# Pooled attention and routed experts on one core: 64-row transposes in two row groups, and indirect transfers tied to the place of the products

## The chip, the cores and the metric

One Trainium2 chip, of which the kernel uses one core. The metric is the device time of one execution in microseconds (us). The engines are TensorE (PE, with its weight loads listed apart as PEld), VectorE (DVE), ScalarE (ACT), GpSimd (POOL) and SyncE (SP, which only issues transfers).

## The reference

```
q_pool = q.reshape(8, 8, 576, 2, 64).mean(axis=3)          # 8 batches, 8 heads, 1152 rows of 64
scores = q_pool @ k.T / 8;  attn = softmax(scores)
x      = (attn @ v) -> [4608 tokens, 512]                  # 8 batches x 576, heads side by side
e, g   = argmax and top softmax of x @ w_gate              # 8 experts
out[t] = g[t] * relu(x[t] @ w1[e]) @ w2[e]                 # w1 512x1024, w2 1024x512
```

## The kernel before, in words

**Attention.** The work goes by batch (8), by pair of heads (4) and by half of the 576 pooled rows (2). `load_pair` brings K, Q and V of a pair (`kn`, `qn`, `vn`), ACT reorders K (`kp`), POOL adds neighbouring rows of Q (`qp`, L465), and `piece` turns both on PE. A pair has four pieces: five tiles of Q, four of K, four of K, and one of each. Each takes the only slot of the PSUM kind `bank`, turns 128x128 (K) or 96x128 (Q) tiles through the identity, and is copied out by ACT into `kT` (L489) and `qT` (L493). `scores` multiplies `kT` by `qT` for nine chunks of K, each into one of two PSUM slots of the kind `st` (L521, four tile products of 64x64 at a time), DVE takes them to `s` (L525), ACT makes the exponential (L553), POOL folds the chunks for the sums (L599), `values` multiplies `s` by V (L624). Score and value products run "tiled", in 64x64 pieces of the array; PE's transposes of K and Q and the gate products are not.

**Routing.** At the end of a batch each token's expert is found, and POOL writes the tokens' entries into one list for each expert with six indirect transfers (`enlist`, `lists<-re,di`, L799).

**MoE.** 16 lists of tokens are worked off, the first two of 384 tokens ("early") from what the first seven batches found, so that their tokens are gathered while the last batch is still in the attention. POOL gathers 32 tokens at a time (`gather`, `xr` or `xq` `<-x_runs,ix`, L899, 148 in all), DVE weighs them (L1056, L1057) and transposes them (L1060), ACT and DVE split them into a high and a low part (L1064, L1019), PE does the first products (L1113, `ph`) and the second ones (L1141, `py`), ACT copies `y`, and POOL scatters it to the output (`out_dram<-y,rec`, L1148, 41).

**Order.** None of this is written in the order in which it runs. Each step is added to a `Flow` with an engine, a length, a due key, what it follows and what buffers it holds; `Flow.emit` walks these with a model of time, and `trace` writes the instructions of all engines in the order that it finds. The tile framework adds the waits that the data need, and it takes two indirect scatters to the same output for dependent unless they are declared free of each other. An engine works off its own instructions in the written order and waits at each for its semaphores.

Of the kernel before, what the change touches and what calls it, by code (L numbers as in the profile page):

```python
# [25 lines left out]
COLS, QUADS = 1, 2  # L26
# [38 lines left out]
SWITCH = 150  # L65

# [22 lines left out]
class Flow:  # L89


    def __init__(self, room=None, old=(), new=(), swap=None):

        self.room, self.steps = room, []
        self.old, self.new, self.swap = set(old), set(new), swap

    def add(self, eng, ns, fn, key=0.0, after=(), holds=(), tiled=False, late=0):
# [5 lines left out]
        step = [key, len(self.steps), eng, ns, fn, list(holds), 0, [], True, list(after), tiled, late]  # L103
# [6 lines left out]
    def carry(self, eng, ns, fn, key, after, holds, move, late=0):  # L110

        s = self.add(eng, ns, fn, key, after, holds)
        return s and self.add("DMA2" if eng == "POOL" else "DMA", move, lambda: None, key, [s], holds, late=late + (1200 if eng == "POOL" else 0))

    def emit(self):
# [12 lines left out]
        tiled, blocked = False, {}  # L128
# [23 lines left out]
        while left:  # L152
            moved = False
            for e in free:
# [44 lines left out]
                free[e] = start + s[3]  # L199
                heapq.heappush(events, (free[e] + OWN[e], s[1], 0, s))  # L200
# [29 lines left out]
    def trace(self, order):  # L230

        todo = sum(self.uses(s, self.old) for s in order)
        while order:
# [5 lines left out]
            for s in order:  # L239
# [6 lines left out]
                s[4]()  # L246
# [6 lines left out]
def kernel(  # L253
# [166 lines left out]
    def act(n):  # L420
        return 110 + 0.833 * n
# [23 lines left out]
    def load_pair(o, f, key, b, hp):  # L445
# [3 lines left out]
        qn = tile_of(o, "qn", [QP, 2, NJ, 2, D], pool=o.ld)  # L449
        x.vn = vn = tile_of(o, "vn", [P, 2, NC, D], bufs=3, pool=o.rt)  # L450
        kp = tile_of(o, "kp", [P, NC, 2, D], pool=o.ld)
        qp = tile_of(o, "qp", [QP, NJ, 2, D], pool=o.ld)
# [8 lines left out]
        q0 = f.carry("SP", 480, lambda: load(qn.t, qb), key + K_LOAD, (), [qn], 2600)  # L461
# [11 lines left out]

        def piece(key, ks, qs, after):

            pt = bank(o)
            nk, n = len(ks) * P, len(ks) * P + len(qs) * QP

            def turn():
                for i, c in enumerate(ks):  # L480
                    nc.tensor.transpose(pt.t[:, i * P:(i + 1) * P], kp.t[:, c].rearrange("p h d -> p (h d)"), ident)
                for i, j in enumerate(qs):
                    nc.tensor.transpose(pt.t[:, nk + i * QP:nk + (i + 1) * QP], qp.t[:, j].rearrange("p h d -> p (h d)"),
                                        ident[:QP, :QP])

            s = f.add("PE", 0.9 * n, turn, key, after, [pt, *([kT, kp] if ks else []), *([qT, qp] if qs else [])])
            o.turned.append(s)
            if ks:
                e = f.add("ACT", act(nk) - 44, lambda: nc.scalar.copy(kT.t[:, ks[0] * P:ks[0] * P + nk], pt.t[:, :nk]),  # L489
                          key, done(s), [pt, kT])  # L490
                x.k.update((c, done(e)) for c in ks)
            if qs:
                e = f.add("ACT", act(n - nk) - 44, lambda: nc.scalar.copy(qT.t[:, qs[0] * QP:qs[0] * QP + n - nk], pt.t[:, nk:n]),  # L493
                          key, done(s), [pt, qT])
                for half in range(qs[0] * 2 // NJ, 2):
                    x.q[half] = x.q.get(half, []) + done(e)

        piece(key, [], [0, 1, 2, 3, 4], done(q1))
        piece(key + 2, [0, 1, 2, 3], [], done(k1))
        piece(key + 4, [4, 5, 6, 7], [], done(k1))  # L500
        piece(key + 6, [8], [5], done(k1, q1))
        return x

    def scores(o, f, key, x, half, step=None):
# [8 lines left out]
        for c in range(NC):  # L513
            pt = hold_of("st", lambda h: o.ps_s.tile([P, 2, 512], F32, **h.own("st")))

            def product(c=c, pt=pt):

                for i in range(2):
                    for h in range(2):
                        up, to = slice(h * D, (h + 1) * D), slice(i * D, (i + 1) * D)  # L520
                        nc.tensor.matmul(pt.t[to, h, :HQ], x.kT.t[up, c * P + i * D:c * P + (i + 1) * D], x.qT.t[up, cols],  # L521
                                         start=True, stop=True, tile_position=(up.start, to.start))

# [763 lines left out]
```

## Time and profile before

| what | value |
|---|---|
| median of 3 runs | 1312.04 us (1309.75 to 1315.79) |
| the profiled execution | 1304.89 us, its span 1303.3 us, mean granted PE clock 0.967 |
| PE busy | 1222.0 us, 94% of the span |
| POOL busy | 862.1 us, 66% |
| DVE busy | 771.5 us, 59% |
| ACT busy | 637.5 us, 49% |
| attention, routing and early lists | about 0 to 755 us of the span |
| MoE | about 755 to 1303 us |

Busy PE time is an average over two parts with different limits, so the prediction reads stretches of the span. Ends of matmuls are modelled and overlap the next start, so the step from one start to the next is the measure of what PE work costs.

### The profile page before, as it was taken

To read this page: it belongs to the slowest core of one execution; us is meant where nothing else is said; L and a number is where in the kernel's file an instruction comes from. 1 tells how busy PE (TensorE), PEld (TensorE's weight loads), DVE (VectorE), ACT (ScalarE), POOL (GpSimd) and SP (SyncE) were. 2 spreads that over 40 slices of the span, in tenths; PEclk is the share of its full clock that TensorE was granted. 3 is DMA by queue.
4 is the path that set the end of the run, shared out by engine and by line. 5 is a ranking of instruction groups with operands and counts; after the bars stand their busy time and mean duration, and the time that the engine had idled before them with its cause. 6 is when DMAs were issued, how large, how long until landed. Compare 5 with 4: busy or idle time off the path is not lost. (4 is left out here: it accounts for less than half of the span.)

```text
span 1303.3 us, 32720 instructions
## 1 busy us (share of the span) xinstructions
PE 1222.0 (94%) x13677; PEld 844.5 (65%) x13677; DVE 771.5 (59%) x2080; ACT 637.5 (49%) x832; POOL 862.1 (66%) x539
## 2 busy tenths in 40 slices
PE   7999999999999999999999598898689889999995
PEld 3555555555555555555555157797578779899895
DVE  5777777767767768768776067663334435425440
ACT  4666666656666666666574046332223323424440
POOL 2999799798998998998992701577475755300110
PEclk8999999999999999999999699999798899999998
DMA  5523233323333333323324205652333434414330
GB/s 165 140 82 93 87 93 94 95 74 105 98 92 110 78 93 104 85 89 98 91 77 152 50 2 140 211 167 57 108 109 96 124 91 128 128 69 146 104 100 19
DMA packets 73517, 131.75 MB, mean 101 GB/s; under 512 B 9347, under 2 KB 32799, under 8 KB 73360
## 3 DMA queue, kind: packets, MB, share of 16 engines
q1 hardware_dynamic: 62528, 109.89, 28.8%
q0 software_dynamic: 9744, 19.64, 5.4%
q8 instruction: 110, 1.80, 0.7%
q14 instruction: 47, 0.39, 0.1%
q10 hardware_dynamic: 1088, 0.03, 0.1%
HBM read 108.75 MB, written 21.02 MB: 100 GB/s over the span
## 5 line engine op out<-in xcount | busy, mean ns | idle before, releaser
L525 DVE TENSOR_SCALAR_CACHE_REDUCE s<-st 128x576 f32<-128x576 f32 x576 | 424.5, 754 | 166.9 <-PE st L521 162.6
L553 ACT ACTIVATE s<-s,bias 128x1728 f32<-128x1728 f32 x192 | 325.3, 1733 | 172.5 <-DVE bias L549 168.2
L521 PE MATMUL st<-qT,kT 64*64 64x288 f32 x4608 | 374.8, 413 | 10.1 <-DVE bias L549 4.9
L624 PE MATMUL pa<-s,vn 64*64 64x288 f32 x4608 | 357.8, 405 | 3.6 <-issue 3.5
L521 PEld LDWEIGHTS st<-qT,kT 64*64 64x64 f32 x4608 | 160.5, 133 | 135.4 <-DVE s L525 30.0
L624 PEld LDWEIGHTS pa<-s,vn 64*64 64x64 f32 x4608 | 171.8, 133 | 102.9 <-issue 9.5
L599 POOL TENSOR_TENSOR fold<-s 128x1728 f32<-128x1728 f32 x58 | 224.3, 3875 | 14.3 <-ACT s L553 9.3
L599 POOL TENSOR_TENSOR fold<-fold,s 128x1728 f32<-128x1728 f32 x58 | 224.1, 3873 | 1.1
L1113 PE MATMUL ph<-xh,w1h 128*128 128x384 f32 (+6 forms) x512 | 162.9, 318 | 31.7 <-DVE hl L1121 22.0
L1113 PE MATMUL ph<-xl,w1h 128*128 128x384 f32 (+6 forms) x512 | 161.2, 315 | 0.7 <-DVE xl L1019 0.6
L1113 PE MATMUL ph<-xh,w1l 128*128 128x384 f32 (+6 forms) x512 | 160.8, 314 | 0.0
L1148 POOL DMA_INDIRECT out_dram<-y,rec x41 | 44.0, 1072 | 174.2 <-ACT y L1153 158.3
L899 POOL DMA_INDIRECT xr<-x_runs,ix x104 | 111.4, 1072 | 65.7 <-issue 26.8
L1121 DVE SCALAR_TENSOR_TENSOR hl<-ph,hh 128x384 fp32r<-128x384 f32 (+5 forms) x100 | 54.8, 550 | 148.3 <-ACT hh L1119 114.0
L1119 ACT ACTIVATE hh<-ph 128x384 fp32r<-128x384 f32 (+5 forms) x100 | 48.8, 488 | 187.4 <-PE ph L1113 139.6
L1141 PE MATMUL py<-w2h,hh 128*128 128x512 f32 x328 | 129.4, 394 | 4.0 <-issue 4.0
L1141 PE MATMUL py<-w2l,hh 128*128 128x512 f32 x328 | 129.0, 393 | 0.0
L1141 PE MATMUL py<-w2h,hl 128*128 128x512 f32 x328 | 128.9, 393 | 0.0
L1113 PEld LDWEIGHTS ph<-xh,w1h 128*128 128x128 f32 x512 | 100.8, 197 | 37.0 <-DVE hl L1121 25.0
L799 POOL DMA_INDIRECT lists<-re,di x48 | 44.7, 932 | 99.0 <-DVE di L759 65.7
L1113 PEld LDWEIGHTS ph<-xl,w1h 128*128 128x128 f32 x512 | 101.0, 197 | 1.9 <-DVE xl L1019 0.9
L1113 PEld LDWEIGHTS ph<-xh,w1l 128*128 128x128 f32 x512 | 100.9, 197 | 0.0
(176 smaller groups left out, 1372.6 us busy)
## 6 DMA issues: line engine op xcount, KB each, us to landing
raw<-in_moe_w_dram SPq DMA_DIRECT2D x80, 512.0 KB
kn<-in_k_dram SPq DMA_DIRECT2D x32, 576.0 KB
qn<-in_q_dram SPq DMA_DIRECT2D x32, 576.0 KB
vn<-in_v_dram SPq DMA_DIRECT2D x32, 576.0 KB
x_runs<-row SPq DMA_DIRECT2D x24, 396.0 KB
xr<-x_runs,ix POOLq DMA_INDIRECT x104
x_runs<-empty SPq DMA_DIRECT2D x4, 297.0 KB
lists<-re,di POOLq DMA_INDIRECT x48
```

The source lines that it names most:

```text
L521: nc.tensor.matmul(pt.t[to, h, :HQ], x.kT.t[up, c * P + i * D:c * P + (i + 1) * D], x.qT.t[up, cols], start=True, stop=True, tile_position ...
L525: nc.vector.tensor_scalar(s.t[:, c], pt.t[:, :, :HQ], -SCALE, None, op0=ALU.mult, op1=ALU.min, accum_out=mx.t[:, c:c + 1],)
L553: nc.scalar.activation(s.t[:, c0:c0 + n], s.t[:, c0:c0 + n], AF.Exp, bias=bias.t, scale=-1.0)
L599: add = lambda to, a, b: nc.gpsimd.tensor_tensor(to, a, b, ALU.add)
L624: nc.tensor.matmul(pa.t[cs, i, :HQ], x.vn.t[up, h, c, :], s.t[up, c, h], start=c == 0, stop=c == NC - 1, tile_position=(up.start, cs.start))
L799: ins = nc.gpsimd.indirect_dma_start(out=lists, out_offset=bass.IndirectOffsetOnAxis(ap=di.t[:, j:j + 1], axis=0), in_=re.t[:, j, :], in_o ...
L899: nc.gpsimd.indirect_dma_start(out=x.xr[i // NQD].t[:, i % NQD, :], out_offset=None, in_=xg, in_offset=bass.IndirectOffsetOnAxis(ap=x.ix.t ...
L1113: nc.tensor.matmul(view()[:, i, :], a[:, c, fp], b[:, c, :n], start=c == 0 and k == 0, stop=c == NDC - 1 and k == 2)
L1119: a = f.add("ACT", act(nb * n) - 44, lambda fs=fs, view=view: nc.scalar.activation(hidden(m)[0][:, fs, :n], view(), AF.Relu), at - 20, don ...
L1121: d = f.add("DVE", dve(nb * n), lambda fs=fs, view=view: nc.vector.scalar_tensor_tensor(hidden(m)[1][:, fs, :n], view(), 0.0, hidden(m)[0] ...
L1141: nc.tensor.matmul(py.t, a[:, c, hs], b[:, c % 2, :], start=c == 0 and k == 0, stop=c == NFC - 1 and k == 2)
L1148: nc.gpsimd.indirect_dma_start(out=out, out_offset=bass.IndirectOffsetOnAxis(ap=x.re.t[:up, r:r + 1], axis=0), in_=y.t[:up], in_offset=Non ...
```

## The change

It has three parts, and the order of all engines is planned anew with them.

1. K and Q are turned in tiles of 64 rows. The upper 64 rows go through row group 0 of the array and the lower ones through row group 64, each into a PSUM bank of its own of one `st` slot. A pair now has two pieces: one tile of K with all six of Q, and the other eight of K; `bank` is no longer used for it. The copies of ACT are one of 1024 columns and one of 128 for K, one of 576 for Q. Q is loaded in two transfers of 64 rows (rows 32 to 63 twice), and its tiles have 128 partitions.
2. List scatters, gathers and output scatters become "paced". The planner lets the next one start only 1300 ns (`CALM`) after the end of the one before, in its own model of time, and `in_step` makes each wait, on the chip, for the last PE instruction written ahead of it.
3. The scatters to the output are declared independent of each other.

```
-            pt = bank(o)
+            pt = hold_of("st", lambda h: o.ps_s.tile([P, 2, 512], F32, **h.own("st")))
...
-                for i, c in enumerate(ks):
-                    nc.tensor.transpose(pt.t[:, i * P:(i + 1) * P], kp.t[:, c].rearrange("p h d -> p (h d)"), ident)
+                for n, c in enumerate(ks):
+                    for i in range(2):
+                        up = slice(i * D, (i + 1) * D)
+                        nc.tensor.transpose(pt.t[:, i, n * D:(n + 1) * D], kp.t[up, c].rearrange("p h d -> p (h d)"),
+                                            ident[up, up], tile_position=(up.start, 0))
+                for n, j in enumerate(qs):
+                    for i, w in enumerate((QH, D)):
+                        up = slice(i * D, i * D + w)
+                        to = (nk + n) * D + (D - QH) * (1 - i)
+                        nc.tensor.transpose(pt.t[:, i, to:to + w], qp.t[up, j].rearrange("p h d -> p (h d)"),
+                                            ident[up, up], tile_position=(up.start, 0))
...
-        piece(key, [], [0, 1, 2, 3, 4], done(q1))
-        piece(key + 2, [0, 1, 2, 3], [], done(k1))
-        piece(key + 4, [4, 5, 6, 7], [], done(k1))
-        piece(key + 6, [8], [5], done(k1, q1))
+        piece(key, [8], [0, 1, 2, 3, 4, 5], done(k1, q1))
+        piece(key + 4, [0, 1, 2, 3, 4, 5, 6, 7], [], done(k1))
...
+                    if s[12] and now < calm:
+                        skipped.append(s)
+                        continue
...
+                if s[12]:
+                    calm = free[e] + CALM
...
+                made = s[4]()
+                if s[2] == "PE" and hasattr(made, "ins"):
+                    self.pe = made
+                if s[12] and self.pe is not None:
+                    self.pace(made, self.pe)
...
+        def in_step(ins, pe):
+            tc.add_manual_dep(ins.ins, pe.ins.name, mybir.DependencyInfo(
+                mybir.DependencyClass.Sync, mybir.DependencyReason.DATA), reason="no sooner than its place in the order")
...
+                    for other in written:
+                        tc.declare_no_dep(ins.ins, other.ins, reason="a token stands in one list once")
+                    written.append(ins)
```

The first place is PE's order while a pair is turned. Before, a row of the order stands for the steps of a kind and tile (`st` scores, `pa` values, `m` a turned piece, `sums` the totals of the fold):

```order
L521 MATMUL st_515<-qT_411,kT_355 64x288 x4
L521 MATMUL st_521<-qT_411,kT_355 64x288 x4
L481 MATMUL m_527<-ident,kp_441 128x128 x4
L624 MATMUL pa_387<-s_279,vn_229 64x288 x4
L521 MATMUL st_540<-qT_411,kT_355 64x288 x4
L521 MATMUL st_546<-qT_411,kT_355 64x288 x4
L481 MATMUL m_552<-ident,kp_441 128x128 x4
L608 MATMUL sums_560<-fold_417,ones_73 32x288 x4
L521 MATMUL st_566<-qT_411,kT_355 64x288 x4
L521 MATMUL st_573<-qT_411,kT_355 64x288 x4
L481 MATMUL m_579<-ident,kp_441 128x128
L483 MATMUL m_579<-ident,qp_462 128x96
```

The same work of PE after the change, at the end of a piece with Q (its last transpose) and at the piece of eight K tiles behind it:

```order
L505 MATMUL st_2402<-ident,qp_2315 128x64
L631 MATMUL sums_1907<-fold_2209,ones_73 32x288 x4
L499 MATMUL st_2422<-ident,kp_2143 128x64 x16
L647 MATMUL pa_2359<-s_2080,vn_1558 64x288 x8
L543 MATMUL st_2454<-qT_2120,kT_2118 64x288 x4
L647 MATMUL pa_2359<-s_2080,vn_1558 64x288 x4
L543 MATMUL st_2469<-qT_2120,kT_2118 64x288 x4
L647 MATMUL pa_2359<-s_2080,vn_1558 64x288 x4
L543 MATMUL st_2479<-qT_2120,kT_2118 64x288 x4
```

The K piece now follows the Q piece closely, both stand in `st` slots, and two scores follow on the values instead of standing between the pieces.

The second place is POOL's order at the gathers of the first early list (`ix` is the list's index, one tile `xr` holds four gathers), with the semaphores that each waits for. Before:

```order
L899 DMA xr_9284<-x_runs,ix_9205 128x132 [waits DMASW6_49]
L899 DMA xr_9284<-x_runs,ix_9205 128x132 [waits DMASW7_49]
L899 DMA xr_9284<-x_runs,ix_9205 128x132 [waits DMASW0_49]
L899 DMA xr_9284<-x_runs,ix_9205 128x132 [waits DMASW1_49]
L899 DMA xr_9361<-x_runs,ix_9205 128x132 [waits DMASW2_49]
```

After the change, the same gathers:

```order
L924 DMA xr_9709<-x_runs,ix_9581 128x132 [waits DMASW6_49,PE_49]
L924 DMA xr_9709<-x_runs,ix_9581 128x132 [waits DMASW7_49,PE_49]
L924 DMA xr_9709<-x_runs,ix_9581 128x132 [waits DMASW0_49,PE_49]
L924 DMA xr_9709<-x_runs,ix_9581 128x132 [waits DMASW1_49,PE_49]
L924 DMA xr_9834<-x_runs,ix_9581 128x132 [waits DMASW2_49,PE_49]
```

Each gather has gained a wait for PE, for an instruction further on in PE's order than that of the gather before it.

The third place is POOL's order in the MoE, around the second output scatter of the first early list (`rec_1`). Before:

```order
L899 DMA xr_10432<-x_runs,ix_10206 128x132 [waits DMASW5_49]
L899 DMA xq_10498<-x_runs,ix_10206 128x132 [waits DMASW6_49]
L1148 DMA out_dram<-y_10502,rec_1_9219 4608x512 [waits DMASW7_49,Activation_49]
L899 DMA xq_10498<-x_runs,ix_10206 128x132 [waits DMASW0_49]
L899 DMA xq_10498<-x_runs,ix_10206 128x132 [waits DMASW1_49]
L899 DMA xq_10498<-x_runs,ix_10206 128x132 [waits DMASW2_49]
L1148 DMA out_dram<-y_10551,rec_1_9219 4608x512 [waits DMASW7_49,DMASW3_49,Activation_49]
L899 DMA xr_10572<-x_runs,ix_10206 128x132 [waits DMASW4_49]
```

After the change, at the first scatters of the same list (`ix_10693` belongs to the first list found after the last batch):

```order
L924 DMA xq_10873<-x_runs,ix_10693 128x132 [waits PE_49,Pool_49]
L924 DMA xq_10873<-x_runs,ix_10693 128x132 [waits PE_49] x2
L924 DMA xr_10964<-x_runs,ix_10693 128x132 x4
L1175 DMA out_dram<-y_10858,rec_1_9596 4608x512 [waits Activation_49]
L1175 DMA out_dram<-y_10910,rec_1_9596 4608x512 [waits DMASW6_49,Activation_49]
```

POOL stood at the gathers of the fourth list (`ix_10206`, the second one found after the last batch) when the first early list was written out; now it stands at those of the third, whose last gathers have no wait of their own for PE, since no PE instruction stands between them in the written order. The second scatter has lost its wait for the first one's transfer.

## Rows read from the trace of the kernel before

**Rows 1.** From the page: the engines' busy time over the whole span, with the share of the span and the number of instructions.

```profile
PE 1222.0 (94%) x13677; PEld 844.5 (65%) x13677; DVE 771.5 (59%) x2080; ACT 637.5 (49%) x832; POOL 862.1 (66%) x539
```

**Rows 2.** Busy time by engine in one stretch, a batch of the attention's steady state (start:end and length in us, then each engine with its count of instructions, TensorE's granted clock, share and rate of the DMA engines).

```profile
403.10:493.70 90.60, 90.41 (x1380) 51.70 (x1372) 66.52 (x200) 58.16 (x72) 85.09 (x35) 1.00 0.34 94
```

**Rows 3.** The timeline of POOL in that batch (start, duration, engine, line, operation, tiles; in brackets the idle time before it and what ended it).

```profile
416.79 0.92 POOL L799 DMA_INDIRECT lists<-re,di  x1 [3.65 <-DVE top L546]
...
419.70 3.89 POOL L599 TENSOR_TENSOR fold<-s 128x1728 f32<-128x1728 f32 x1 [0.77 <-PE st L521]
```

**Rows 4.** The timeline of PE around three of the four pieces in which K and pooled Q are turned. A group of 8 records is one step of four tile products on each half of the array; ends are modelled, so starts are compared.

```profile
299.68 0.66 PE L624 MATMUL pa<-s,vn 64*64 64x288 f32 x8
...
303.07 0.66 PE L521 MATMUL st<-qT,kT 64*64 64x288 f32 x8
303.67 0.66 PE L481 MATMUL m<-ident,kp 128*128 128x128 f32 x4
304.26 1.20 PE L521 MATMUL st<-qT,kT 64*64 64x288 f32 x16
...
403.78 0.63 PE L483 MATMUL m<-ident,qp 96*128 96x96 f32 x5
...
430.07 0.66 PE L521 MATMUL st<-qT,kT 64*64 64x288 f32 x8
430.67 0.33 PE L481 MATMUL m<-ident,kp 128*128 128x128 f32 x1
...
431.01 0.71 PE L521 MATMUL st<-qT,kT 64*64 64x288 f32 x8
```

**Rows 5.** The timeline of TensorE's weight loads at the first of these pieces, with the next score products' behind it, and the group of the former over the span (busy time, mean ns of one, idle time before them and what ended it).

```profile
303.67 0.42 PEld L481 LDWEIGHTS m<-ident,kp 128*128 128x128 f32 x4 [0.44 <-issue]
304.25 0.21 PEld L521 LDWEIGHTS st<-qT,kT 64*64 64x64 f32 x8 [0.17 <-issue]
...
L481 PEld LDWEIGHTS m<-ident,kp 128*128 128x128 f32 x288 | 31.6, 141 | 47.4 <-issue 34.7 <-ACT qT L493 3.6 <-ACT xT L628 2.8
```

**Rows 6.** Groups of instructions by line: ACT's copies out of PSUM behind the turning and its exponentials.

```profile
L553 ACT ACTIVATE s<-s,bias 128x1728 f32<-128x1728 f32 x192 | 325.3, 1733 | 172.5 <-DVE bias L549 168.2 <-DVE xr L1056 3.3
L489 ACT COPY kT<-m 128x512 f32<-128x512 f32 (+1 forms) x96 | 45.6, 475 | 33.9 <-PE m L481 20.3 <-PE m L483 13.4 <-issue 0.2
L493 ACT COPY qT<-m 128x480 f32<-128x480 f32 x64 | 25.4, 397 | 20.6 <-PE m L483 20.4
```

**Rows 7.** The timeline of POOL and PE at the six list scatters of batch 6, and before it at three of batch 0.

```profile
142.87 0.92 POOL L799 DMA_INDIRECT lists<-re,di  x1 [0.30 <-issue]
143.00 0.72 PE L521 MATMUL st<-qT,kT 64*64 64x288 f32 x8
...
688.78 0.92 POOL L799 DMA_INDIRECT lists<-re,di  x1 [3.64 <-DVE top L546]
...
692.95 0.70 PE L594 MATMUL sums<-s,ones 128*32 128x288 f32 x4 [0.45 <-issue]
...
694.89 0.92 POOL L799 DMA_INDIRECT lists<-re,di  x1 [0.30 <-issue]
...
697.24 0.79 PE L594 MATMUL sums<-s,ones 128*32 128x288 f32 x8 [0.79 <-issue]
```

**Rows 8.** The first and the last of the 24 gathers of the two early lists on POOL, PE's records at the same time, and PE's busy time in that stretch.

```profile
715.36 1.06 POOL L899 DMA_INDIRECT xr<-x_runs,ix  x1 [19.54 <-DMA raw<-in_moe_w_dram]
...
745.36 1.00 POOL L899 DMA_INDIRECT xr<-x_runs,ix  x1 [0.30 <-issue]
...
722.46 0.71 PE L594 MATMUL sums<-s,ones 128*32 128x288 f32 x4 [0.71 <-issue]
...
749.74 1.24 PE L521 MATMUL st<-qT,kT 64*64 64x288 f32 x8 [4.93 <-DVE bias L549]
...
718.00:746.00 28.00, 16.46 (x68) 4.67 (x62) 0.73 (x4) 0.00 (x0) 21.58 (x22) 0.70 0.24 54
```

**Rows 9.** Two stretches of the MoE by engine, and for the first of them what PE and DVE waited for (engine, line, releaser: us in total, times, longest).

```profile
800.00:1080.00 280.00, 245.84 (x1255) 219.81 (x1255) 135.49 (x254) 85.98 (x135) 176.05 (x212) 0.93 0.42 123
1080.00:1280.00 200.00, 200.00 (x1199) 183.01 (x1198) 86.35 (x122) 74.54 (x114) 38.64 (x41) 1.00 0.33 107
...
PE ph L1113 <- DVE hl L1121: 22.0, 9, 8.8
...
DVE xr L1056 <- DMA xr<-x_runs,ix: 48.1, 12, 11.9
```

**Rows 10.** The timeline at one list's tokens in the MoE, from a gather to its weighing, and the groups of the three operations behind.

```profile
841.87 1.01 POOL L899 DMA_INDIRECT xr<-x_runs,ix  x1 [0.30 <-issue]
...
844.57 0.17 DVE L1056 TENSOR_TENSOR xr<-xr,li 128x16 f32<-128x16 f32 x1 [7.08 <-DMA xr<-x_runs,ix]
844.78 0.69 DVE L1057 TENSOR_TENSOR xr<-xr 128x512 f32<-128x512 f32 x1
...
L1060 DVE STREAM_TRANSPOSE xt<-xr 128x512 f32<-128x512 f32 (+2 forms) x27 | 18.1, 680 | 0.0
L1064 ACT CAST xh<-xt 128x512 fp32r<-128x512 f32 (+3 forms) x41 | 22.1, 576 | 8.9 <-DVE xt L1060 4.6 <-DVE xl L1019 2.7 <-issue 0.8
L1019 DVE TENSOR_TENSOR xl<-xt,xh 128x512 fp32r<-128x512 f32 (+3 forms) x41 | 24.6, 632 | 0.8 <-ACT xh L1064 0.7
```

**Rows 11.** The timeline of POOL at the end of the program.

```profile
1291.17 0.87 POOL L1148 DMA_INDIRECT out_dram<-y,rec  x1 [4.44 <-ACTq L1226]
```

More of the change, by code (lines that the diff above doesn't have):

```diff
@@ L25 @@
 UNITS = 4
-COLS, QUADS = 1, 2
+COLS, QUADS, ROWS = 1, 2, 3
 KT_BUFS = 2
@@ L89, with __init__, add @@
 class Flow:
-    def __init__(self, room=None, old=(), new=(), swap=None):
+    def __init__(self, room=None, old=(), new=(), swap=None, pace=None):
         self.room, self.steps = room, []
+        self.pace, self.pe = pace, None
         self.old, self.new, self.swap = set(old), set(new), swap
-    def add(self, eng, ns, fn, key=0.0, after=(), holds=(), tiled=False, late=0):
+    def add(self, eng, ns, fn, key=0.0, after=(), holds=(), tiled=False, late=0, paced=False):
         if self.room is None:
@@ L102, in add @@
             h.left += 1
-        step = [key, len(self.steps), eng, ns, fn, list(holds), 0, [], True, list(after), tiled, late]
+        step = [key, len(self.steps), eng, ns, fn, list(holds), 0, [], True, list(after), tiled, late, paced]
         for a in after:
@@ L108, in add, with carry @@
         return step
-    def carry(self, eng, ns, fn, key, after, holds, move, late=0):
-        s = self.add(eng, ns, fn, key, after, holds)
+    def carry(self, eng, ns, fn, key, after, holds, move, late=0, paced=False):
+        s = self.add(eng, ns, fn, key, after, holds, paced=paced)
         return s and self.add("DMA2" if eng == "POOL" else "DMA", move, lambda: None, key, [s], holds, late=late + (1200 if eng == "POOL" else 0))
@@ L460, in load_pair @@
         k0 = f.carry("SP", 480, lambda: load(kn.t, kb), key + K_LOAD, (), [kn], 2600)
-        q0 = f.carry("SP", 480, lambda: load(qn.t, qb), key + K_LOAD, (), [qn], 2600)
+        q0 = f.carry("SP", 960, lambda: [load(qn.t[i * D:(i + 1) * D], qb[i * BL:i * BL + D]) for i in range(2)],
+                     key + K_LOAD, (), [qn], 2600)
         x.v = f.carry("SP", 480, lambda: load(vn.t, heads(v, b, hp).rearrange("h (p c) d -> p h c d", p=P)),
@@ L487, in piece @@
+            s = f.add("PE", 27 * 2 * (nk + len(qs)), turn, key, after, [pt, *([kT, kp] if ks else []), *([qT, qp] if qs else [])], ROWS)
             o.turned.append(s)
             if ks:
-                e = f.add("ACT", act(nk) - 44, lambda: nc.scalar.copy(kT.t[:, ks[0] * P:ks[0] * P + nk], pt.t[:, :nk]),
-                          key, done(s), [pt, kT])
+                e = f.add("ACT", act(nk * P), lambda: nc.scalar.copy(
+                    kT.t[:, ks[0] * P:(ks[0] + nk) * P].rearrange("p (c r i) -> p r c i", r=2, i=D),
+                    pt.t[:, :, :nk * D].rearrange("p r (c i) -> p r c i", i=D)), key, done(s), [pt, kT])
@@ L501, in load_pair @@
-        piece(key + 6, [8], [5], done(k1, q1))
+                e = f.add("ACT", act(NQ), lambda: nc.scalar.copy(
+                    qT.t.rearrange("p (j r i) -> p r j i", r=2, i=QH),
+                    pt.t[:, :, nk * D:(nk + NJ) * D].rearrange("p r (j i) -> p r j i", i=D)[:, :, :, D - QH:]),
+                    key, done(s), [pt, qT])
+                x.q.update((half, done(e)) for half in range(2))
+        piece(key, [8], [0, 1, 2, 3, 4, 5], done(k1, q1))
+        piece(key + 4, [0, 1, 2, 3, 4, 5, 6, 7], [], done(k1))
```

50 lines of the change are left out of this document (26 added, 24 removed).

## The prediction

> **What bounds the kernel now.** I read the page first, then the attention and the MoE apart, since PE's 94% [rows 1] is an average over two limits.
>
> In the attention's steady state a batch takes 90.60 us, and PE is busy for 90.41 of it at the full granted clock (1.00, 2.4 GHz), POOL for 85.09 [rows 2]. PE is the limit, and POOL stands close behind it: its only idle times that aren't its own issuing are 3.65 and 0.77 us [rows 3], so POOL alone would need 90.6 − 4.4 = 86.2 us. ACT (58) and DVE (67) are far off [rows 2]. The reader is to see that what PE saves beyond some 4.4 us a batch, nobody gets.
>
> Near the end of the attention the picture breaks twice. While POOL issues six list transfers 1.22 us apart, PE does its totals with gaps of 0.45 to 0.79 us that nothing in the profile explains [rows 7]. With 24 gathers 1.30 us apart, PE goes on with such gaps (0.71 after the first long record) until in 28 us it has issued 68 records, at a granted clock of 0.70, and then waits 4.93 us for a bias [rows 8]. Three transfers in a row do no harm: PE starts the next group at 143.00, while the third is under way [rows 7].
>
> In the MoE's first 280 us PE is busy for 245.84 at a granted clock of 0.93, in the next 200 for all of it at 1.00 [rows 9]. The lost time of the first part is 22.0 us for `hl`, 9 times, up to 8.8, and `hl` is late because DVE, which makes it, stands 48.1 us at the rows of gathers (`xr`, 12 times) with `hl` queued behind [rows 9].
>
> **The change, term by term.** The base is the profiled execution, 1304.89 us, with 1303.3 us of span; it lies 0.5% under the median of 1312.04, so the sum is scaled by 1.0055 at the end.
>
> *Turning.* Steps of score and value groups come every (303.07 − 299.68)/7 = 0.485 us [rows 4]. Between the group ahead of a piece and the one behind it pass 304.26 − 303.07 = 1.19 for four K tiles and 431.01 − 430.07 = 0.94 for one of each; less 0.485, the pieces cost 0.705 and 0.455; the one of five Q tiles, whose record has 0.63 where K's has 0.66, I put at 0.675 [rows 4]. A pair has two of the first and one of each other: 2.54 us, and 10.2 a batch. The MATMULs of four tiles are shown with 0.66 and of one with 0.33 [rows 4], so a 128-column transpose adds 0.11 and a piece has some 0.265 of its own for leaving and entering the tiled products. After: 15 pairs of 64-column transposes in two pieces. If the two row groups run side by side, as four tile products do now (a group of eight is shown with 0.66, while the next starts 0.485 later [rows 4], far less than eight in turn would take), that is 15 × 0.055 + 2 × 0.265 = 1.355, a gain of 1.19 a pair and 4.7 a batch. One after the other it is 30 × 0.055 + 0.53 = 2.18, a gain of 0.36. I take the first, since the products of this kernel on other quarters of the array do overlap.
>
> What could hold it is the weights: 30 loads a pair instead of 15. The loads of whole tiles come 0.42 us for 4, at 141 ns each over the span [rows 5], so their starts are at most (0.42 − 0.14)/3 = 0.093 us apart; 30 of these one by one would cost 2.79 + 0.53 = 3.32 us a pair, 0.78 more than before and 25 us in 32 pairs. Two half loads at once would make it 1.93. In the scores, loads into different quarters go by 8 in 0.21 us [rows 5], 0.026 us each, which speaks for the lower number; both are bounds of the range. The Trainium skill, "TensorE: Matmul & The Clock Gate", section "LDWEIGHTS (loading the stationary operand)", says that loading goes with the columns of the stationary operand and not with its rows, so halving the rows would halve nothing; its figure, columns/1.2 in ns, gives an estimate of 107 ns a load, 3.74 us a pair and 38 us more over 32 pairs. This trace's loads, at no more than 93 ns apart, lie below that figure, and no run here shows 64-row loads of 128 columns.
>
> PE would come down to 85.9 a batch, below POOL's 86.2. POOL's gaps don't all close, because its transfers and folds wait for others: I take 87.8, a little over a third of the way from its floor to the 90.6 of now. That gives 2.8 us a batch in the six batches of steady state, 17; the first and the last batch, which wait for loads and for routing as well, I put at 3 and 4. Together **−24**; ends: −9 (0.36 × 4 × 6 with nothing more) and −34 (1.19 × 32, less 4).
>
> *What the turn now holds.* A piece takes one of two `st` slots until ACT has copied it, and ACT may stand in an exponential of 1.73 us [rows 6]. Meanwhile scores have one slot: an estimate of 1.5 us each (the product's 0.66 [rows 4], DVE's take of some 0.7, of which its 66.5 us a batch [rows 2] hold 72, and their hand-over) instead of two groups' 0.97. Value groups hide it: 18 per pair, 8.7 us at 0.485. Without that cover it is two pieces × about 0.55, 1.1 us a pair, which eats the whole gain. ACT's copies stay off the path: the same 1728 columns a pair go in three copies instead of five, so no more than the 45.6 + 25.4 = 71.0 us of now [rows 6]. The second load of Q is one more issue on SP, whose transfers stand far ahead of POOL's add.
>
> *Pacing, up to the MoE.* The bursts cost about 5 us at the lists of batch 6 (PE's totals crawl from 692 to 698 [rows 7]) and about 30 at the gathers (28 us from 718 with some 3 us of work in them, then 4.93, and a clock that has fallen [rows 8]). After, the written order has a gather every 1 to 3 us of PE's work, and each waits for PE's place there, so a PE that stalls holds the next gather back. That the last six of the 24 are not held matters little: they stand just ahead of the first product of the MoE, whose records are long and few. I take **−33** of 35; ends: −16, if each of the 24 spaced transfers still costs one such gap of 0.72 (17 us), and −35.
>
> *Pacing, in the MoE.* Here the change costs. From a gather to the product that needs it: 1.30 between gathers, 844.57 − 841.87 = 2.70 to the rows, 0.17 and 0.69 on DVE, 0.68 for the transpose, 0.58 on ACT, 0.63 on DVE [rows 10]. In the written orders, PE already stands at the product of a list when some of its gathers are not issued: five of the third list, three of the 7th, 9th and 15th, two of the 11th; the 5th has some 5 us in hand. With n gathers left a wait is n × 1.30 + 2.7 + 2.75 − 1.1 (an estimate of the work that PE still has in hand there): 10.8 for five, 8.2 for three, 6.9 for two, 2.6 for the 5th list. The sum is 10.8 + 3 × 8.2 + 6.9 + 2.6 = 45, and after each such wait a stretch at the lower clock of about 3, 15 in all. Before, the same part lost 34 us idle [rows 9] and, by its granted clock, about 14 in its work: 48. So **+13**; ends: −25 (most of the 48 go because rows no longer block DVE out of turn) and +25.
>
> *Scatters free of each other.* The last one of before waited 4.44 us for its issue, long after its data [rows 11]; nothing is queued behind them that PE needs. 0 ± 1.
>
> Sum: 1304.9 − 24 − 33 + 13 = 1260.9; × 1.0055 = **1268 us** (1250 to 1285 by itself).
>
> **Rivals**, each worked out on the same base and scaled.
> - *The MoE gains instead.* DVE waits 48.1 us for rows in the written place [rows 9]; if gathers in step with PE end those, −15 in place of +13: 1233, scaled 1240. Against it speak the gathers that stand behind their product in the order.
> - *The turn gains little* because the row groups run in turn, POOL keeps its gaps, or scores want the slot: −9 instead of −24: 1276, scaled 1283.
> - *Spaced transfers still stall PE*, one gap of 0.72 each: 1277, scaled 1285, and with little gain of the turn about 1300. The three transfers of batch 0 [rows 7] speak against it.
> - *Loads bound the turn*, serial at 0.093: +25 instead of −24, 1310, scaled 1317, no change. By the Trainium skill's figure above (same page and section) it would be +38, 1323, scaled 1330. The loads of quarters, 8 in 0.21 us, speak against it.
> - *Rows are late at every list* (this ends slower). Gathers in step with PE can't run ahead of it, so a delay of one list isn't made up in the next. With 13 lists behind the third at the longest wait of before, 8.8, and 3 of low clock, it is 153 instead of 48: 1304.9 − 57 + 105 = 1353, scaled 1360. It decides from 8.1 us a list: 13 × 8.1 = 105, which is 48 + 57. Six lists of the sum have such a wait, so it would need twice as many.
>
> **How the numbers follow.** Forecast 0.45; the MoE gains 0.15; little gain of the turn 0.15; spaced transfers stall 0.10; loads bound 0.05; late at every list 0.10. Time 1268, from the likeliest. The range leaves out the last two and the fringes of the others: 1228 to 1304, from a gaining MoE with 12 us more to a turn and a pacing that both fall short. A measurement of this kernel tells about 0.5% from no change, 1305.5 to 1318.6. Faster: the first four, less 0.01 at their edge, 0.84; same: half of the loads' case and part of a milder lateness, 0.05; slower: 0.11.
>
> **What would show it.** Right: a batch of 87 to 89 us with POOL at 98% of it; pieces of K with 0.7 us for eight tiles; no gap of 0.7 us in PE around the early gathers and a granted clock near 1.00 there; PE waits at the start of lists 3, 7, 9, 11 and 15 of 7 to 11 us, ended by DVE. Wrong: a batch still at 90 with PE full (loads or row groups in turn), `st` waits for ACT's copies, gaps at each spaced gather, or MoE waits at nearly every list.

## The result, and the profile after

The changed kernel takes about the same time, half a percent more: 1318.23 us median (10 runs) against 1311.85, a ratio of 1.0054 (95% interval 1.0033 to 1.0074). The ratio is that of the fast runs, without one run of each kernel that stood far off (2701 and 1409 us). Its profiled execution took 1319.63 us with a span of 1318.1, where the one of before took 1304.89.

The page of the changed kernel: busy time by engine, and the granted clock in 40 slices.

```profile
PE 1191.4 (90%) x14157; PEld 829.4 (63%) x14157; DVE 768.3 (58%) x2080; ACT 628.4 (48%) x768; POOL 878.7 (67%) x539
...
PEclk9999999999999999999999898799997979799898
```

PE has 31 us less to do than in [rows 1], and the span is 15 us longer. The clock row shows where: slices of 7 to 9 fill the last 40%, the MoE. Stretches of the changed kernel: a batch of the attention, the 28 us of [rows 8], and the MoE from its first to its last product.

```profile
394.63:484.46 89.83, 87.69 (x1437) 49.42 (x1433) 65.36 (x200) 56.81 (x64) 85.15 (x35) 1.00 0.38 104
718.00:746.00 28.00, 28.00 (x440) 16.60 (x433) 13.61 (x37) 12.73 (x11) 12.13 (x13) 1.00 0.13 31
750.46:1303.85 553.39, 471.80 (x2548) 424.71 (x2548) 236.48 (x399) 170.27 (x270) 234.18 (x258) 0.91 0.36 106
```

The same stretch of the MoE in the kernel before:

```profile
790.05:1289.85 499.80, 464.99 (x2547) 418.74 (x2548) 229.73 (x393) 169.69 (x270) 215.68 (x254) 0.96 0.38 116
```

The gate products of the eight batches (L698, after: L722) mark the way. The seventh of them begins at 676.34 before and at 664.09 after (12.3 us gained), the eighth at 794.51 and 755.32 (26.9 more), and the MoE's first product at 790.05 and 750.46: 39.6 us are gained by then. Steady batches take 89.8 instead of 90.6. The early gathers no longer stop PE: it is busy for 28.00 of 28 us at full clock, where [rows 8] has 16.46 at 0.70. Then the MoE takes 553.4 instead of 499.8 us, 53.6 more: PE is idle for 81.6 instead of 34.8, and its busy time is 6.8 longer at a mean granted clock of 0.91 instead of 0.96. What PE waits for in the MoE of the changed kernel (us in total, times, longest):

```profile
PE ph L1138 <- ACT xh L1089: 68.3, 7, 22.4
PE m L1026 <- DVE f L1025: 8.7, 1, 8.7
PE py L1167 <- ACT y L1185: 4.3, 1, 4.3
```

The waits for `hl` of [rows 9] are gone (1.0 us); in their place stand seven for the tokens of a list.

### The profile page after: what moved, and what is told of

Its sections match the earlier page's. It is cut to its first block, busy times and chain, and to the rows that moved or that the text cites. A ratio compares the mean times of both kernels' runs of the same rounds, so it can differ in the third digit from the quotient of the medians.

```text
span 1318.1 us, 33770 instructions
## 1 busy us (share of the span) xinstructions
PE 1191.4 (90%) x14157; PEld 829.4 (63%) x14157; DVE 768.3 (58%) x2080; ACT 628.4 (48%) x768; POOL 878.7 (67%) x539
## 5 line engine op out<-in xcount | busy, mean ns | idle before, releaser
L548 DVE TENSOR_SCALAR_CACHE_REDUCE s<-st 128x576 f32<-128x576 f32 x576 | 417.2, 753 | 166.9 <-PE st L543 166.0
L576 ACT ACTIVATE s<-s,bias 128x1728 f32<-128x1728 f32 x192 | 321.0, 1730 | 174.7 <-DVE bias L572 174.3
L543 PE MATMUL st<-qT,kT 64*64 64x288 f32 x4608 | 360.0, 411 | 18.6 <-DVE s L548 13.8
L647 PE MATMUL pa<-s,vn 64*64 64x288 f32 x4608 | 346.1, 405 | 0.2
L1138 PE MATMUL ph<-xh,w1h 128*128 128x384 f32 (+6 forms) x512 | 165.6, 323 | 69.3 <-ACT xh L1089 68.3
L647 PEld LDWEIGHTS pa<-s,vn 64*64 64x64 f32 x4608 | 167.0, 133 | 93.3 <-DVE xT L653 6.7
L924 POOL DMA_INDIRECT xr<-x_runs,ix x104 | 118.1, 1136 | 131.6 <-PE ph L1138 43.6
L1138 PE MATMUL ph<-xl,w1h 128*128 128x384 f32 (+6 forms) x512 | 165.1, 322 | 1.0 <-DVE xl L1044 0.8
L1138 PE MATMUL ph<-xh,w1l 128*128 128x384 f32 (+6 forms) x512 | 163.6, 320 | 0.0
L924 POOL DMA_INDIRECT xq<-x_runs,ix x44 | 52.7, 1197 | 62.0 <-PE py L1167 42.4
```

Of the source, the lines that this page charges most:

```text
L543: made = nc.tensor.matmul(pt.t[to, h, :HQ], x.kT.t[up, c * P + i * D:c * P + (i + 1) * D], x.qT.t[up, cols], start=True, stop=True, tile_p ...
L548: nc.vector.tensor_scalar(s.t[:, c], pt.t[:, :, :HQ], -SCALE, None, op0=ALU.mult, op1=ALU.min, accum_out=mx.t[:, c:c + 1],)
L576: nc.scalar.activation(s.t[:, c0:c0 + n], s.t[:, c0:c0 + n], AF.Exp, bias=bias.t, scale=-1.0)
L647: made = nc.tensor.matmul(pa.t[cs, i, :HQ], x.vn.t[up, h, c, :], s.t[up, c, h], start=c == 0, stop=c == NC - 1, tile_position=(up.start, c ...
L924: return nc.gpsimd.indirect_dma_start(out=x.xr[i // NQD].t[:, i % NQD, :], out_offset=None, in_=xg, in_offset=bass.IndirectOffsetOnAxis(ap ...
L1138: made = nc.tensor.matmul(view()[:, i, :], a[:, c, fp], b[:, c, :n], start=c == 0 and k == 0, stop=c == NDC - 1 and k == 2)
```

## The experiments

One fact comes first. The runs stood on several chips, and the kernel before took 1312 us in the first runs, whose chip isn't on record, 1247.7 and 1245.2 on two others (called quiet below), and 1300.4, 1307.5 and 1299.1 on three more. Each of these five chips was used for one set of runs only, so what belongs to the chip and what to the occasion isn't separated; "chip" stands for both. So ratios go against the kernel before on the same chip, and profiles are compared by stretches. The times expected of `e1` to `e4` were meant for the first chip. "MoE" is the time from the first `ph` product to the last `py` product. In the runs with a change of their own the edit is one to the changed kernel unless said otherwise.

**The change taken apart.** `e1` keeps the turning alone: `paced=True` is taken from the list scatters, the gathers and the output scatters, and the latter depend on each other again.

```
-            outs.append(f.carry("POOL", 1230, lambda j=j: enlist(j), at + (K_PUT if b is None or b < B - 2 else 0) * j / NJ, done(p, *hold), [di, re], 40, paced=True))
+            outs.append(f.carry("POOL", 1230, lambda j=j: enlist(j), at + (K_PUT if b is None or b < B - 2 else 0) * j / NJ, done(p, *hold), [di, re], 40))
...
-                if f.room is not None:
+                if False:
```

> Part 1 of the change alone (64-row turning); no transfer is paced, the scatters depend on each other as before. My theory: the turn gives what the changed kernel's trace shows for the attention (3.8 us in the first batch, 5.4 in the second, 0.8 in each later one, some 14 in all), the bursts stay, and the MoE's products keep their 500 us: about 1298. Rival, the turn's new order is what cost the MoE its 54 us: about 1350. If the list scatters' waits for PE hold POOL back in the steady state, a batch falls here to 87 to 88 instead of 89.8, and the time to about 1285.

0.9952 (0.9934 to 0.9971): 1242.9 us. MoE 480.5, the first product at 747.5. The turn's new order costs the MoE hardly anything (the kernel before has 477.9 on a quiet chip, see below); a batch takes 89.33, hardly less than with the pacing.

`e2` keeps the pacing and the free scatters, with `load_pair` of before.

> Parts 2 and 3 alone (pacing, in step, free scatters) with the turning of before. My theory, the pacing costs the MoE 54 us and gives 27 back before it: about 1339, with PE waits of 10 us and more at some five lists. Rival, the MoE's loss comes with the turn: about 1285.

1.0643 (1.0621 to 1.0664): 1327.9 us, MoE 546.6, PE waiting 77.5 us in seven waits for a list's tokens, the longest 27.9. The pacing makes the loss, without the turn.

`e3` paces only what runs ahead of the MoE: `paced=True` becomes `paced=b != B - 1` at the list scatters and `paced=early` at the gathers, and is taken from the output scatters.

```
-            f.carry("POOL", 1300, scatter, at, done(a), [y, x.re], 1200, paced=True)
+            f.carry("POOL", 1300, scatter, at, done(a), [y, x.re], 1200)
```

> The changed kernel, but paced are only the list scatters of batches 0 to 6 and the 24 early gathers; the last batch's list scatters, the 124 other gathers and the output scatters are free of the pace. My theory: the 40 us up to the first product stay and the MoE returns to about 500 us: about 1272. Rival, the loss in the MoE comes from the turn's or the free scatters' order: about 1318.

1.0036 (1.0018 to 1.0054): 1252.0 us, MoE 488.9. Of the 66 us less than 1318, 64 are the MoE's. That the kernel before is not beaten here goes back to the chip, see below.

`e4` spaces nothing (`-CALM = 1300`, `+CALM = 0`); `e5` drops the wait for PE:

```
-                if s[12] and self.pe is not None:
-                    self.pace(made, self.pe)
```

> The changed kernel with CALM = 0: nothing is spaced in the order, yet every indirect transfer still waits for the PE instruction ahead of it. If the spacing in the written order makes the gathers late: the MoE back at 500 to 510 us, the bursts partly back, about 1285. If the wait for PE itself does it: about 1318, with PE waits of about 10 us at the same lists.

> The changed kernel with the spacing of the written order (CALM = 1300) but without the wait for PE. My theory: the MoE's loss needs both, an order in which gathers stand late and a wait that keeps POOL from running ahead of it; then the MoE is at about 490 us, as with the wait alone, and the whole is within 1% of the run with CALM = 0 (1258 where before takes 1248). Rival, the written order alone does it, since gathers stand behind other work of POOL: about 1315, PE waits of 10 us and more.

`e4`: 1.0085 (1.0052 to 1.0118), 1257.9 us, MoE 491.6. `e5`: 1.0254 (1.0219 to 1.0288), 1279.8 us, MoE 519.4, with waits of 17.8 us at the third list and 5.5 to 7.2 at the 7th, 9th, 11th and 15th. Against the 478 of the kernel before on such a chip, the wait alone costs 14, the spaced order alone 41, both 75 (the turn and the free scatters are in all three): the larger part is the written order, and the wait keeps POOL from making up for it. My expectation for `e5`, as cheap as `e4`, was wrong, and so was its rival of 1315.

**The chip.**

> The kernel before itself, for a profile on the chip on which the other runs of this call stand. In the call ahead of this one, on another chip than that of the first profile, it took 1247.7 us instead of 1312. Theory, the two chips differ at the bursts: here the 24 early gathers let PE go on (the last two batches' logits 91 instead of 118 us apart), and the MoE's products take about 480 instead of 500 us, which would be 47 of the 64 us. Rival, the whole program runs faster: the batches of the steady state then are shorter than 90.6 us too.

> The changed kernel itself beside the one before. If the stall at the bursts is the chip's, the pacing has nothing to give back on a chip without it: about 1316 here too, which is 5% slower than 1248. If the chip is like the first, before 1312 and this 1318.

Before took 1246.9 here (ratio 1.0002 to the runs beside it), and the changed kernel 1318.2: 1.0565 (1.0538 to 1.0592), on this chip a loss of 5.6%. The changed kernel thus takes the same on both kinds of chip; it is the kernel before that varies. On this chip PE's busy time under the same gathers, still 1.30 us apart:

```profile
711.00:739.00 28.00, 28.00 (x460) 16.12 (x458) 19.58 (x57) 11.87 (x9) 21.53 (x22) 1.00 0.34 104
```

That is 28.00 of 28 us at full clock, with 460 records where [rows 8] has 68. Batch 7 takes 84.7 instead of 118.2 us and the MoE 477.9 instead of 499.8: 33 + 22 of the 58 us between the two spans, and the steady batch is nearly equal (90.3 and 90.6). The stall that the pacing takes away doesn't exist on such a chip.

`e10` is the turn alone, with the early gathers in step but nothing spaced (`paced=early` in `gather` alone, `CALM = 0`).

> The 64-row turning, and of the pacing only that the 24 early gathers wait for their place on PE, with nothing spaced (CALM = 0) and no freedom of the scatters. The early gathers have 20 to 38 us in hand, so I expect it at the turning alone, 1241 to 1245 where before takes 1246. If holding these gathers costs the first list, 10 us more.

0.9961 (0.9930 to 0.9991), 1297.1 us, on a chip where before takes 1300.4. POOL's early gathers in it, and a record of PE among them:

```profile
727.72 1.00 POOL L924 DMA_INDIRECT xr<-x_runs,ix  x1 [0.30 <-issue]
729.64 1.00 POOL L924 DMA_INDIRECT xr<-x_runs,ix  x1 [0.92 <-PE st L543]
730.94 0.99 POOL L924 DMA_INDIRECT xr<-x_runs,ix  x1 [0.30 <-issue]
...
754.02 0.40 PE L543 MATMUL st<-qT,kT 64*64 64x288 f32 x1 [0.69 <-issue]
```

The gathers wait for PE and are still 1.3 to 1.9 us apart; batch 7 takes 105.7 us, less than the 118 of before and more than the 91.2 of the changed kernel. So the wait alone spares PE only in part. My expectation, 1241 to 1245, was for a quiet chip. Batches 2 to 6 take 92 to 94 us, where the turn alone has 89.33 on a quiet chip. One place where they lose it follows four list scatters 1.22 us apart (414.53 to 418.19):

```profile
417.27 1.15 PE L647 MATMUL pa<-s,vn 64*64 64x288 f32 x16
421.02 2.20 PE L543 MATMUL st<-qT,kT 64*64 64x288 f32 x16 [2.60 <-DVE s L548]
```

From these values to the next scores pass 3.75 us; at the same place of `e1`, behind four list scatters just as close, it is 0.97. Whether the distance alone, without the wait for PE, spares PE on such a chip was not run.

**Which spacing.**

> The changed kernel with CALM = 400 instead of 1300. My theory: from the last batch on, 171 paced transfers (6 list scatters, 124 gathers, 41 output scatters) are written 1.31 + 1.30 = 2.61 us apart, 446 us in all, nearly the 478 us that the MoE's products take in the kernel before; so the order has POOL as its limit and no gather gets ahead. At 400 it is 1.71 us, 292 in all: the MoE falls from 553 to about 495, the time to about 1263 where before takes 1246. Rival, any spacing together with the wait for PE does it: within 15 us of 1318.

> The changed kernel with CALM = 1300, but the 41 output scatters neither spaced nor made to wait for PE. The paced stream of the MoE is then 130 transfers, 339 us. If the full stream is what makes the gathers late, the waits of 10 us at the 7th, 9th, 11th and 15th list go and the one of 22 us at the 3rd, where POOL's index work stands between the gathers, stays at least in part: MoE about 505, time about 1270. If the waits go with the spacing of each gather, about 1315.

`e8` (`+CALM = 400`): 0.9560 (0.9511 to 0.9609), 1242.6 us, MoE 472.8. `e9` (`paced=True` taken from `scatter` alone): 0.9661 (0.9613 to 0.9710), 1255.8 us, MoE 487.9. In `e9` PE's waits for tokens at the 7th to 15th list are gone, 16.0 us at the third list stay, and 9.9 for `hl` stand at the start of the MoE. Both came out lower than expected, by 20 and 14 us, in the direction of the full stream.

> The changed kernel with CALM = 700: the 171 paced transfers of the MoE take 171 x 2.01 = 344 us of POOL's plan. If the loss comes when the planned stream fills the MoE's 478 us (446 at 1300, 292 at 400), 700 is still free of it: the MoE at 475 to 490 us, total 1243 to 1260. Rival, each us of spacing makes each list late in proportion: of the 80 us between 400 and 1300 a third, MoE about 500, total about 1268.

> The changed kernel with CALM = 1000: 171 x 2.31 = 395 us of POOL's plan, beside which POOL has its index work to do. By the theory of the full stream the waits begin between here and 1300: MoE 490 to 520, total 1260 to 1290. By proportion: two thirds of the 80 us, MoE about 526, total about 1295.

At 700: 0.9673 (0.9616 to 0.9731), 1258.2 us, MoE 484.9. At 1000: 0.9776 (0.9718 to 0.9834), 1271.9 us, MoE 508.9, with these waits of PE for tokens:

```profile
PE ph L1138 <- ACT xh L1089: 30.2, 7, 9.4
```

From 400 to 700, 1000 and 1300 the MoE grows by 12, 24 and 44 us: not in proportion, but ever steeper as the planned stream (292, 344, 395, 446 us) fills the time of the products. Both values lie in the ranges of the full stream, below those of proportion. `e9` fits in: its 130 transfers are 339 us of stream at full distance, and its MoE of 487.9 lies beside the 484.9 of 344 us. Below that the stream is not what counts: with nothing spaced, `e4` has a longer MoE (491.6) than 400 has, and PE waits there for `hl`. Each order is planned anew; what in it does that is not shown.

> The kernel before, for a profile on this call's chip, beside the next three. Either the gathers at 1.30 us stop PE, as in the first profile (batch 7 takes 118 us, total about 1300 to 1312), or they don't (85 us, 1246).

> The changed kernel with CALM = 400 once more, on another chip. My theory: its time hardly depends on the chip, 1240 to 1246, since its transfers don't stop PE and its gathers come in time; so it wins 4 to 5% where before takes 1300 and 0 to 0.5% where before takes 1246. Rival, it won only because of that chip: then it stands at some other distance from before.

> Pacing with CALM = 400, in step, and free scatters, with the turning of before. Beside the run ahead of it the difference is the turn alone in a paced order: 10 to 14 us slower if the turn gives what the attention showed (0.8 to 1.3 us in six batches, 3.8 and 5.4 in the first two).

Before: 1310.3 us, batch 7 121 us, much as in the first profile (118). `e8b`: 0.9493 (0.9470 to 0.9515), 1244.2 us, on a second chip as on the first. `e12` (`e2` with `CALM = 400`): 0.9665 (0.9633 to 0.9696), 1265.4 us. The turn is worth 21 us in this order, more than expected; 9.5 of them lie ahead of the first product, the other 12 in a MoE of 484.3 instead of 472.4, whose order is planned anew too. Early gathers of `e8b` on POOL, and its MoE with PE's waits:

```profile
716.45 1.01 POOL L924 DMA_INDIRECT xr<-x_runs,ix  x1 [0.63 <-PE st L543]
718.16 1.01 POOL L924 DMA_INDIRECT xr<-x_runs,ix  x1 [0.70 <-PE st L543]
719.88 1.01 POOL L924 DMA_INDIRECT xr<-x_runs,ix  x1 [0.71 <-PE st L543]
```

```profile
753.81:1226.22 472.41, 453.46 (x2549) 410.19 (x2549) 229.82 (x392) 168.24 (x269) 219.04 (x254) 0.98 0.39 123
...
PE ph L1138 <- ACT xh L1089: 6.7, 1, 6.7
PE ph L1138 <- DVE hl L1147: 6.1, 4, 2.7
PE py L1167 <- DVE hl L1147: 5.4, 1, 5.4
```

The gathers stand 1.7 us apart instead of 1.30, PE isn't stopped by them (batch 7 takes 88.8 us), and 18 us of waits are left in the MoE. This version beats the kernel before on the two chips where it ran, by 4.4 and 5.1%. The changed kernel was not run on these two; it took 1318 on one chip of either kind. On a chip where before takes 1246 the version was not run; if it kept its 1243 there, that would be no difference to speak of.

**Where the turn's gain went.** `e7` adds the neighbouring rows of Q on DVE instead of POOL, in `e3`:

```
-        e, eng, ns = ("DVE", nc.vector, dve) if opening else ("POOL", nc.gpsimd, pool)
+        e, eng, ns = "DVE", nc.vector, dve
```

> The kernel with pacing up to the MoE (1252 where before takes 1248), with the adding of neighbouring rows of Q moved from POOL to DVE for every pair: 7.3 us less a batch on POOL, about 3.8 more on DVE. If POOL is what holds the batch at 89.8 us, it falls to PE's 87 to 88, and the time by some 12. If the two PSUM slots of the scores and DVE's takes of them hold it, it stays at 89.8 or grows by up to 3.

1.0317 (1.0290 to 1.0345), 1287.5 us. A batch of it:

```profile
417.51:512.03 94.52, 87.27 (x1445) 49.99 (x1441) 77.73 (x206) 57.45 (x65) 80.83 (x31) 1.00 0.37 98
```

POOL has 4.3 us less than in the changed kernel's batch, DVE 12.4 more (I had expected 3.8), and the batch takes 94.5. With less on POOL it gets no shorter; but as DVE has more to do at the same time, the run doesn't clear POOL by itself. Better evidence is what PE's weight loads wait for in the changed kernel's batch (394.63 to 484.46): DVE's takes of the scores, or POOL's fold.

```profile
PEld st L543 <- DVE s L548: 9.9, 20, 0.9
...
PEld sums L631 <- POOL fold L622: 1.7, 3, 0.7
```

The stretch at a piece of the changed kernel, on PE:

```profile
416.14 1.15 PE L543 MATMUL st<-qT,kT 64*64 64x288 f32 x16
417.69 1.40 PE L543 MATMUL st<-qT,kT 64*64 64x288 f32 x16 [0.40 <-DVE s L548]
419.29 1.40 PE L543 MATMUL st<-qT,kT 64*64 64x288 f32 x16 [0.21 <-DVE s L548]
420.90 0.71 PE L543 MATMUL st<-qT,kT 64*64 64x288 f32 x8 [0.21 <-DVE s L548]
421.54 0.69 PE L631 MATMUL sums<-fold,ones 128*32 128x288 f32 x8
422.17 0.27 PE L499 MATMUL st<-ident,kp 64*128 64x64 f32 x2
422.28 0.54 PE L505 MATMUL st<-ident,qp 48*128 48x48 f32 x12
422.64 0.67 PE L499 MATMUL st<-ident,kp 64*128 64x64 f32 x16
423.24 1.20 PE L647 MATMUL pa<-s,vn 64*64 64x288 f32 x16
```

Ahead of the turning seven scores stand in a row, 416.14 to 421.54, 0.77 us each instead of 0.485, and each group of them but the first waits for DVE's take of an `st` slot. Over a batch, from each start to the start of what follows, the turning falls from 8.3 to 4.4 us, while the scores grow from 37.6 to 39.7 and the rest by 0.8 (the kernel before from the profile below): of 3.8 us saved some 0.9 remain. `e11` puts the four old pieces of the kernel before into an `st` slot:

```
-            pt = bank(o)
+            pt = hold_of("st", lambda h: o.ps_s.tile([P, 2, 512], F32, **h.own("st")))
```

> The kernel before with its four pieces of 128-row transposes, but drawn in an st slot instead of the bank slot. It measures the slot alone. Theory, the slot is what takes back the turning's gain (3.8 us of PE a batch saved, 0.95 gained): a batch grows by 2 to 4 us, the time to about 1265. Rival, scores wait for DVE's takes because PE is now ahead of DVE: the batch stays at 90.3 and the time at 1246.

> The kernel before with its pieces in an st slot, beside a profile of before on the same chip. On the last chip its batches took 94.3 to 96.3 us and PE 41.75 us a batch for its scores. If the slot does that, the batches of before on this chip are 3 to 5 us shorter and its scores take 37 to 38 us. Rival, the chip does it: before shows the same.

1.0237 (1.0168 to 1.0305) and 1.0207 (1.0157 to 1.0257). On the second chip, beside each other, a batch of the kernel before and the loads of its scores that waited for DVE:

```profile
494.31:585.02 90.71, 90.44 (x1373) 51.62 (x1372) 66.52 (x200) 58.12 (x72) 85.06 (x35) 1.00 0.33 94
...
PEld st L521 <- DVE s L525: 3.5, 12, 0.5
```

and the same with the pieces in `st`:

```profile
512.07:606.41 94.34, 90.07 (x1376) 51.03 (x1372) 65.20 (x200) 57.58 (x72) 85.59 (x35) 1.00 0.33 90
...
PEld st L521 <- DVE s L525: 10.6, 16, 2.5
```

The slot costs 3.6 us in this batch (5.3 in others): PE's loads wait 10.6 instead of 3.5 us for DVE to free a slot, and the scores take 41.6 instead of 37.6 us. A pair holds the slot four times here and twice in the changed kernel, so this shows what the slot does, not how much of it falls to the changed kernel.

## Why the prediction was wrong

The forecast was 1261 for the profiled execution; it took 1319.6. Three terms carried it.

**Turning, −24, measured −12.3.** The price of the transposes was right. From 421.54 to 423.24 lie a group and two pieces: 1.70 − 0.485 = 1.2 us a pair, forecast 1.355, so the row groups do run side by side; the rivals of serial halves and of loads that bound the turn fall. The figure of the Trainium skill from "TensorE: Matmul & The Clock Gate", section "LDWEIGHTS (loading the stationary operand)", is no price of this turn: 30 loads at 107 ns are an estimate of 3.2 us a pair, more than twice the 1.2 measured for all of it. The step that failed is the next one, "PE would come down to 85.9 a batch, below POOL's 86.2". PE did not stop at POOL but at the two `st` slots: the cover by value groups, costed at nothing, doesn't hold where scores follow in a row. The slot was the low end of the text ("1.1 us a pair, which eats the whole gain"), and part of the rival of little gain. `e11` shows that the slot costs, and the waits of PE's loads in the changed kernel, 9.9 us ended by DVE's takes and 1.7 by POOL's fold, show where PE stood. No run gave the 64-row turning a slot outside `st`, so how much of the lost gain the slot explains is not shown. Of the 12.3 us, 3.7 and 5.4 come from the first two batches and some 0.8 from each of the fourth to the seventh. On quiet chips the turn alone gains 12.7 up to the same place and only 4.8 in all (`e1`): its last batch takes 91.1 us where before has 84.7, and its MoE is 2.6 longer.

**Pacing up to the MoE, −33, measured −27.** Right in kind: no gap around the early gathers, clock 1.00. What the text didn't consider is that the stall is not the kernel's alone: on a quiet chip the same gathers at the same 1.30 us stop nothing.

**Pacing in the MoE, +13, measured +53.6.** This term makes the result, and it is the step that failed: its size, not its kind. By its own working it is 45 + 15 − 48 = 12. Measured are 46.8 us more of idle time and 6.8 more of busy time. The price of the clock was right: after the wait at the 7th list the granted clock is 0.50 for some 6 us (1000.4 to 1006.4), which costs the 3 us forecast. The lists at which PE would wait were named rightly: the 3rd with 10.8 forecast and 22.4 measured, the 7th 8.2 and 11.0, the 9th 8.2 and 10.9, the 11th 6.9 and 9.9, the 15th 8.2 and 10.6, the 5th 2.6 and 1.7. Two prices were too low. First, the 2.70 us from a gather to its rows, read at a list where little else moved [rows 10]. At the seventh list, with the weights of the next expert under way on SP's queue:

```profile
979.02 14.11 SPq L1049 DMA_DIRECT2D raw<-in_moe_w_dram  x6
...
989.70 1.05 POOL L924 DMA_INDIRECT xr<-x_runs,ix  x1 [1.13 <-PE py L1167]
991.05 1.01 POOL L924 DMA_INDIRECT xr<-x_runs,ix  x1 [0.30 <-issue]
992.37 1.25 POOL L924 DMA_INDIRECT xr<-x_runs,ix  x1 [0.30 <-issue]
...
998.08 0.17 DVE L1081 TENSOR_TENSOR xr<-xr,li 128x16 f32<-128x16 f32 x1 [4.75 <-DMA xr<-x_runs,ix]
...
1000.43 0.69 PE L1138 MATMUL ph<-xh,w1h 128*128 128x384 f32 x1 [11.00 <-ACT xh L1089]
```

From 992.37 to 998.08 it takes 5.7, and 5.1 to 5.6 at the 9th, 11th and 15th, each time with more than 1 MB moving on SP's queue; at the third list, with nothing on that queue from 851.9 to 854.6, the last gather again takes 2.7. PE stands still with three gathers to go, as counted, and pays 3 us more than forecast. Second, at the third list POOL and PE:

```profile
828.52 1.08 POOL L924 DMA_INDIRECT xr<-x_runs,ix  x1 [0.30 <-issue]
...
832.31 0.77 POOL L908 DMA_DIRECT2D li<-lists  x1 [0.43 <-issue]
833.38 1.08 POOL L924 DMA_INDIRECT xr<-x_runs,ix  x1 [0.31 <-PE py L1167]
834.54 0.32 POOL L918 TENSOR_SCALAR ix<-li,gid 128x12 int32<-128x12 int32 x1
834.83 0.18 POOL L921 COPY rec<-li 32x3 int32<-32x3 int32 x1
836.15 1.05 POOL L921 COPY rec<-li 32x3 int32<-32x3 int32 x3 [1.14 <-DMA xr<-x_runs,ix]
837.47 1.11 POOL L924 DMA_INDIRECT xq<-x_runs,ix  x1 [0.28 <-POOL rec L921]
...
840.29 2.78 POOL L921 COPY rec<-li 32x2 int32<-32x2 int32 x3 [0.70 <-DMA xq<-x_runs,ix]
843.34 1.77 POOL L924 DMA_INDIRECT xq<-x_runs,ix  x1 [0.27 <-POOL rec L921]
...
851.93 1.00 POOL L924 DMA_INDIRECT xr<-x_runs,ix  x1 [0.30 <-issue]
...
856.99 0.69 PE L1138 MATMUL ph<-xh,w1h 128*128 128x384 f32 x1 [22.44 <-ACT xh L1089]
```

PE has stopped at 834.5 (856.99 − 22.44) with eight gathers to go, not five, and the first two are 5.9 us apart, since `ix` and `rec` of a later list stand between them, and `rec` waits for the transfer of the gather ahead. The same work, with loads of later lists (`li`), spreads the gathers before them. Further, 8.7 us for the flag (`f`) behind the last batch's list scatters, which were held back for PE by up to 18.3 us, and 4.3 us for `y` were in no term. The rival "rows are late at every list" did not come true: seven waits, not thirteen, yet 54 us, by longer ones. The cause behind the order, that 171 transfers 2.61 us apart are 446 us of the planned POOL, wasn't seen; it could have been worked out from the 1.31 us of a gather and `CALM`, and `e8`, `e9`, `e13` and `e14` bear it out down to some 340 us of stream.

**Free scatters, 0.** No run had them alone; nothing in the traces speaks against it.

## What to carry to other kernels

Before a stream is spaced, multiply its count by the new distance and hold it against the time of the work that it feeds: 171 transfers at 2.61 us filled this MoE. At 1.71 the same pacing gained 4.4 and 5.1% with the turn, and 3.35% without it, where transfers disturb PE. A slot that is borrowed from a kind that has only two is paid for at the place where its users stand in a row, not on average. And a stall that nothing in the profile explains should be seen on a second chip before its removal is counted as a gain.

## What the hardware showed

The same program took 1299 to 1312 us on some chips and 1245 to 1248 on two others. With its gathers at the same 1.30 us, PE issued 68 records in 28 us on one of the former and 460 on one of the latter. On the first kind PE's records come in small groups with gaps for which the profile names no releaser; transfers 1.7 us apart and in step with PE leave none. What differs between these chips, or the occasions on which they were used, wasn't settled. Two 64-row transposes in different row groups, each to its own PSUM bank, ran side by side: eight K tiles in 0.60 us (422.64 to 423.24), where four took 0.59 [rows 4].
